# Pairing a group's quadrants by row instead of by token half, with a sixth seven-product group in the last pair

## The chip, the core and the metric

The kernel runs on one core of one Trainium2 chip. The metric is the device time of one execution in microseconds; the time before is the median of 3 runs.

## What is computed

A channel attention over 6016 tokens of 256 channels (its 256x256 probabilities are folded into the first weight), then two feed-forward layers with 2048 hidden columns, all in float32:

```python
s = (kn.T @ qn) / tau              # kn, qn: k and q normalized over the tokens
x = v @ softmax(s)                 # 6016 x 256
x = relu(x @ w_in1) ** 2 @ w_out1
out = leaky_relu(x @ w_in2, 0.01) @ w_out2
```

## The kernel before

**Products.** TensorE multiplies in fp32r. A float32 operand is split into a high part, cast by ScalarE, and a low part, which is the difference of operand and high part and is formed by VectorE (`low`, L109). One product is three matmuls (high by low, high by high, low by high; `mm3`, L541), all for one PSUM bank.

**Pairs and units.** The tokens are cut into six pairs of two halves, of 512 tokens each (448 in the fifth pair). In each layer and pair, eight units of 256 hidden columns follow: `(L, p, g)` is layer, pair, unit, and `n` numbers all 96 units. A unit's first multiplication (F1 to F7 in the banks ha and hb, L954) takes seven products instead of eight, as in Winograd's form of Strassen's algorithm. Its results lie in two tiles c, one for each token half, each with two rows of quadrants (fb 0 and 1: the two halves of the hidden columns).

**The second multiplication** has two forms. A plain unit casts each token half, forms its low part, and takes eight products, one for each half, fb and d (the two halves of the output channels). A unit of a seven-product group (`GROUPS`, L52; "S" in the code) takes seven, P1 to P7, and needs differences of quadrants (T1 to T4). P2, P3, P4 and P7 go into the four output banks y, P5 into a bank F (yF in the profile) and P1 and P6 into a bank A (yA). P6 (`yA<-b`) comes only when the P1 of its batch have been taken out of bank A; the batches are three or four units long (L963). Before the change the last pair has five seven-product units, 0 to 4; pairs 4 and 5 of layer 1 have six, and pairs 0 to 4 of layer 2 seven.

**VectorE and ScalarE in a unit of such a group** (`unit`, from L1585): casts and lows of G0 (1024 columns), B22 (512), G1 (1024), T3 (512) and T2 (512), and four differences of 512 columns (L1612): nine operations of VectorE.

**The order of the work** comes from a plan that the kernel makes when it is built (`build`, L987, and `simulate`, L814): every step is a task with an engine, a cost in units of one 512-column matmul, its dependencies and its buffers, and each engine takes the ready task that is due first. A transfer counts in the plan as its size over a rate (40 for the sums and the output) plus 14 units. TensorE (`class PE`, L889) takes the next first product when it is ready, and between two of them a given number of second products, the first ready ones of a list (L913). The list is filled by `mixed_items` (L1706): for unit g first what is late of unit g - 1 (P5, P4, P7), then the unit's own products; at the end of a batch its P6. The plan is written out as one fixed instruction order for each engine; SP's transfers are one queue in this order.

**The end.** In the last pair, the units that are at least two behind the last seven-product unit multiply their second half with the tokens on the output partitions (`second_by_tokens`, L577): 24 matmuls of 256 columns instead of 12 of 512. Before, these are units 6 and 7; unit 5 is plain. The shared sums of the second half must then be turned. `combine_last` (L1802) is issued with unit `BY_TOKENS - 1` (5 before): when the last P6 is done it adds bank A to the sums U, copies y(1,0) out as V, adds P5's bank, and adds the remaining banks; it transposes both results, stores them in DRAM (`ys`, L1834) and loads them back by token (`sums`, L1841). The first two plain products of that unit stand ahead of the late ones, but the one for y(1,0) has to wait for V. `finish_last` (L598) is the last work: four adds of the by-token banks and these sums (L552 in the profile), and three stores of the output. The other half's output is transposed and stored by four transfers (`put`, L621 and L627). The list's last part is sorted so that the by-token matmuls come last (L1872).

Of the kernel before, what the change touches and what calls it, by code (L numbers as in the profile page):

```python
# [19 lines left out]
P = 128  # L20
# [8 lines left out]
def attn_moe_moe2(  # L29
# [22 lines left out]
    GROUPS = {(1, 4): tuple(range(6)), (1, 5): tuple(range(6)), **{(2, p): tuple(range(7)) for p in range(5)}, (2, 5): tuple(range(5))}  # L52
# [43 lines left out]
    wi_d = {(L, g): dram.tile([P, 2, 8, P], F32, name=f"wi{L}_{g}") for L in (1, 2) for g in range(NG)}  # L96
# [27 lines left out]
    class Unit:  # L124
# [6 lines left out]
        def load(self):  # L131
            w, g = WS[self.kind, self.L], self.g
            t = cpool.tile([P, 2, 2 * P, 2], U32, tag="wst", name="wst", bufs=3)
            if self.kind == "i":
                src = w[:, g * 2 * P : (g + 1) * 2 * P].bitcast(U32).rearrange("(k p) f -> p k f", p=P)
            else:
                src = w[g * 2 * P : (g + 1) * 2 * P, :].bitcast(U32).rearrange("(b p) c -> p b c", p=P)
            nc.sync.dma_start(t.rearrange("p a b w -> p a (b w)"), src)
            self.w0, self.w1 = t[:, :, :, 0], t[:, :, :, 1]
# [28 lines left out]
        def into(self):  # L168

            if self.kind == "i" or self.blocks:  # L170
# [5 lines left out]
                return self.x, self.to[:, 0], self.to[:, 1]  # L176
# [21 lines left out]
        def store(self):  # L198
            if self.kind == "o":
                nc.sync.dma_start(wo_d[self.L, self.g], raw(self.to))  # L200
            elif self.L == 2:
                nc.sync.dma_start(wi_d[2, self.g][:, :, 1:], raw(self.to[:, :, 1:]))

    def sums(x, A11=1, A22=2, S1=4, S2=5, S3=6, S4=7):
# [8 lines left out]
    def out_sums(x):  # L213
        return sums(x, A11=2, A22=1, S1=5, S2=6, S3=7, S4=4)
# [355 lines left out]
    def second(n, half, fb, d):  # L570
# [3 lines left out]
        wo = both(wo_t[L, p, g], d, fb)  # L574
        mm3(y, wo, both(g_t[n, half], fb, slice(0, w)), begins((L, p, half, d)))

    def second_by_tokens(n, fb):  # L577
# [5 lines left out]
        for t in range(WIDTH[p] // P):  # L583
            if first:
                by_token.append(y_bank(L, p, 1, t) if t < KC else bank("ce"[t - KC], "y"))
            for m, (a, b) in enumerate(((0, 1), (0, 0), (1, 0))):
# [3 lines left out]
                    wo[:, b, :, fb],  # L590
# [44 lines left out]
    def shared(n, product, bank_key, first):  # L635
# [8 lines left out]
        else:  # L644
            a = both(late_w[n, "S2" if product == "P6" else "S3"], 0)
        x = {"P1": lambda: both(g_t[n, "G0"], 0, sl), "P2": lambda: both(g_t[n, "G0"], 1, sl),
             "P3": lambda: both(b_t[n, "B22"], sl), "P4": lambda: both(g_t[n, "G1"], 1, sl),
             "P5": lambda: both(g_t[n, "G1"], 0, sl), "P6": lambda: both(b_t[n, "T2"], sl),
             "P7": lambda: both(b_t[n, "T3"], sl)}[product]()
# [8 lines left out]

    def result(n, half, w, fb=None):
        c = c_t[n, half]  # L660
        return c[:, :, :w] if fb is None else c[:, fb, :w]
# [208 lines left out]
    KEEP = 8  # L870
    LATE_FIRST = True
# [9 lines left out]
    CONV_BEGIN, CONV_END = 1.4, 4  # L881
    N0 = 4
    FOLD_AFTER = "F1"
# [52 lines left out]
    A = {"A11": 1, "A22": 2, "A12": 3, "S1": 4, "S2": 5, "S3": 6, "S4": 7}  # L936
# [23 lines left out]
    FROM = {"P1": "G0", "P2": "G0", "P3": "B22", "P4": "G1", "P5": "G1", "P6": "T2", "P7": "T3"}  # L960
# [26 lines left out]
    def build(base):  # L987
# [33 lines left out]
        def convert(u, due, loaded=None, first=None, pace=4, begin=0):  # L1021
# [14 lines left out]
            if blocks:  # L1036
                raw_ = Buf("whl", 2, d(4))
                t = T("DVE", 3, d(4), u.high, deps=[t], alloc=raw_, uses=[w, cm])
                for i in range(4):
                    t = T("DVE", 1.1, d(4.2 + i / 10), lambda i=i: (sums if u.kind == "i" else out_sums)(u.x)[i](),  # L1040
                          deps=[t], uses=[raw_])
                to = Buf("wis", 1, d(5))
                t = T("ACT", 4.6, d(5), u.round, deps=[t], alloc=to, uses=[raw_])
                t = T("DVE", 5.2, d(6), u.low, deps=[t], uses=[raw_, to])
# [30 lines left out]
        def fold_sums(n, at_):  # L1075
# [19 lines left out]
            for i in range(4):  # L1095
                a = T("DVE", 1.1, at_ + 11 + i, lambda i=i: r["s"][i](), deps=[a], uses=[xb])
            h_ = T("ACT", 4.6, at_ + 16, lambda: nc.scalar.copy(wi_t[1, 0, g][:, 0], r["x"]), deps=[a], uses=[xb, b])
            lo = T("DVE", 5.2, at_ + 22, lambda: low(wi_t[1, 0, g][:, 1], r["x"], wi_t[1, 0, g][:, 0]), deps=[h_], uses=[xb, b])
            wi_ready[1, 0, g] = wi_ready[n + 1] = lo
            stores["i", 1, g, "s"] = T(  # L1100
                "SP", "wi", at_ + 30, lambda: nc.sync.dma_start(wi_d[1, g][:, :, 1:], raw(wi_t[1, 0, g][:, :, 1:])),
# [247 lines left out]
        def load_wi(n):  # L1349
            L, p, g = units[n]  # L1350
            b = wi_b[n] = Buf("wi", 3, base[n - 2] + 0.5)
            if n < 2 * NG and g < N0:
# [11 lines left out]
                def high():  # L1364
                    nc.scalar.copy(r["w"][:, 0, 4:], r["x"][:, 4:])

                def lows():
                    low(r["w"][:, 1, 4:], r["x"][:, 4:], r["w"][:, 0, 4:])

                def store():  # L1370
                    nc.sync.dma_start(wi_d[L, g][:, :, 4:], raw(r["w"][:, :, 4:]))
# [5 lines left out]
                for i in range(4):  # L1377
                    t = T("DVE", 1.1, e - 20 + i, lambda i=i: r["s"][i](), deps=[t], uses=[xb])
                t = T("ACT", 2.7, e - 10, high, deps=[t], uses=[xb, b])
                wi_ready[n] = T("DVE", 3, e - 5, lows, deps=[t], uses=[xb, b])  # L1380
                stores["i", 1, g, "s"] = T("SP", "fold", e, store, deps=[wi_ready[n]], uses=[b], lat=LOAD)
                return

            def load():
                nc.sync.dma_start(raw(wi_tile(L, p, g)[:, :, 1:]), wi_d[L, g][:, :, 1:])
# [4 lines left out]
        def wo_sums(n, ready, b):  # L1390
# [22 lines left out]
            for i in range(4):  # L1413
                t = T("DVE", 1.1, e + 1, lambda i=i: r["s"][i](), deps=[t], uses=[xb])
# [7 lines left out]
        def load_wo(n):  # L1422
# [24 lines left out]
            def load_s3():  # L1447
                t = late_w[n, "S3"] = wpool.tile([P, 2, 1, P], F32R, tag="ws", name="ws", bufs=3)
                nc.sync.dma_start(raw(t), sums_d[:, :, 7:])
# [3 lines left out]
            def load_s2():  # L1453
# [6 lines left out]
                nc.sync.dma_start(raw(late_w[n, "S2"]), sums_d[:, :, 6:7])  # L1460
# [18 lines left out]
        def unit(n):  # L1479
# [6 lines left out]
            h = lambda i: h_t[n, tags[i]][:, :w]  # L1486
            cb = [Buf("any" if is_mixed(L, p) else "c", 3, t0 + (5, 26)[half]) for half in range(2)]
            for half in range(2):
                cb[half].held = (90, 75)[half] if form == "S" else (55, 45)[half]
                c_tag[n, half] = cb[half]  # L1490
# [3 lines left out]
            def copy(where):  # L1494
# [3 lines left out]
                elif where == "C11":  # L1498
                    new_result(n, 0)
# [9 lines left out]
            def c22():  # L1509
                new_result(n, 1)  # L1510
# [12 lines left out]
            def c11_seeded():  # L1523
                new_result(n, 0)
# [6 lines left out]
            f = {}  # L1531

# [49 lines left out]
            c = lambda half, fb: result(n, half, w, fb)  # L1582
            _, turn_, _ = batch_of(n)

            def cast(name, half):  # L1585
                g_t[n, name] = gpool.tile([P, 2, 2, 512], F32R, tag="g", name="g")
                nc.scalar.copy(g_t[n, name][:, 0, :, :w], result(n, half, w))  # L1587

            def lows(name, half):
                gt = g_t[n, name]  # L1590
                low(gt[:, 1, :, :w], result(n, half, w), gt[:, 0, :, :w])

            def cast1(name, half, fb):
                if name == "B22":
                    b_t[n] = gpool.tile([P, 2, 2, 512], F32R, tag="g", name="b")
                    b_t[n, name] = b_t[n][:, 0]
                elif name == "T3":
                    b_t[n, name] = b_t[n][:, 1]
                elif turn_ > 1:
                    b_t[n, name] = cpool.tile([P, 2, 512], F32R, tag="whl", name="b")  # L1600
                else:
                    if turn_ == 0:
                        b_t[n, "pair"] = cpool.tile([P, 2, 2, 512], F32R, tag="wis", name="b", bufs=1)
                    b_t[n, name] = b_t[n - turn_, "pair"][:, turn_]
                nc.scalar.copy(b_t[n, name][:, 0, :w], c(half, fb))  # L1605

            def low1(name, half, fb):
                b = b_t[n, name]
                low(b[:, 1, :w], c(half, fb), b[:, 0, :w])

            def sub(to, a, b):
                tt(c(*to), c(*a), c(*b), op=ALU.subtract)  # L1612

            b = g_b[n, "G0"] = Buf("g", 4, t0 + 45)
            t = T("ACT", A2, t0 + 45, cast, "G0", 0, deps=[n11, n21], alloc=b, uses=[cb[0]])
            low_of[n, "G0"] = g0 = T("DVE", D2, t0 + 52, lows, "G0", 0, deps=[t], uses=[b, cb[0]])
            b = g_b[n, "B22"] = Buf("g", 4, t0 + 50)
            t = T("ACT", A1, t0 + 50, cast1, "B22", 1, 1, deps=[n12], alloc=b, uses=[cb[1]])
            low_of[n, "B22"] = b22 = T("DVE", D1, t0 + 57, low1, "B22", 1, 1, deps=[t], uses=[b, cb[1]])
            t1 = T("DVE", 3 * s, t0 + 59, sub, (0, 0), (1, 0), (0, 0), deps=[n22, g0], uses=cb)  # L1620
            t3 = T("DVE", 3 * s, t0 + 61, sub, (1, 0), (1, 1), (1, 0), deps=[n12, t1], uses=cb[1:])
            t2 = T("DVE", 3 * s, t0 + 65, sub, (1, 1), (1, 1), (0, 0), deps=[t3, b22], uses=cb)
            t4 = T("DVE", 3 * s, t0 + 67, sub, (0, 1), (0, 1), (1, 1), deps=[t2], uses=cb)
            b = g_b[n, "G1"] = Buf("g", 4, t0 + 74)
            t = T("ACT", A2, t0 + 74, cast, "G1", 0, deps=[t1, t4], alloc=b, uses=[cb[0]])
            low_of[n, "G1"] = T("DVE", D2, t0 + 84, lows, "G1", 0, deps=[t], uses=[b, cb[0]])
            b = g_b[n, "T3"] = g_b[n, "B22"]
# [316 lines left out]
```

## Time and profile before

| | |
|---|---|
| median of 3 runs | 1001.35 us (1000.79 to 1002.28) |
| the profiled execution | 1002.93 us |
| its span, first to last instruction | 1001.1 us |
| busy: TensorE, weight loads, VectorE, ScalarE | 994.6, 837.3, 901.4, 804.4 us |
| matmuls | 4528 |
| bytes moved | 234.97 MB, 235 GB/s over the span |

How to read it: times are microseconds from the span's start. PE is TensorE, PEld its weight loads, DVE VectorE, ACT ScalarE, SPq the queue of transfers that SyncE issues. A busy time is the union of an engine's instructions; matmuls overlap in the pipeline, so their pitch is read from start times. Tiles have the program's names: `y<-g,wo` is a second product, `ha<-x,wi` a first one.

### The profile page before, as it was taken

Reading aid. Unit: us, or ns where it says so; the run is one execution under the profiler, and the core shown is the slowest. Engines: PE = TensorE matmul, PEld = TensorE weight load, DVE = VectorE, ACT = ScalarE, POOL = GpSimd, SP = SyncE. Lnnn points to the kernel's source line nnn. Section 1 sums busy time; section 2 is a strip of 40 time slices with the busy share of each in tenths; the row PEclk is TensorE's granted clock in tenths of the full one; section 3 lists DMA queues with packets and bytes.
Section 4 is the critical chain, followed back from the end, with each engine's and each line's share of the span. In section 5 each row is a group of like instructions: output and inputs, shape, how many; then the busy total and the mean of one; then the engine's idle time right before and its main releaser. Section 6 shows DMA issues by size and latency. Waiting matters only on the chain.

```text
span 1001.1 us, 13148 instructions
## 1 busy us (share of the span) xinstructions
PE 994.6 (99%) x4528; PEld 837.3 (84%) x4528; DVE 901.4 (90%) x1314; ACT 804.4 (80%) x1184; POOL 0.7 (0%) x6
## 2 busy tenths in 40 slices
PE   9999999999999999999999999999999999999998
PEld 7888888887888888998888888888888888998887
DVE  4899999988988977999999999999999999998985
ACT  6799978877878777888898888779788788887773
POOL 0000000000000000000000000000000000000000
PEclk9999999999999999999999999999999999999999
DMA  9786559788978967965665665666577586676553
GB/s 339 281 253 205 200 193 287 266 308 296 332 284 294 318 249 265 316 219 206 223 209 200 229 215 202 201 217 226 172 219 233 182 239 227 210 233 220 195 143 84
DMA packets 160946, 234.97 MB, mean 235 GB/s; under 512 B 53232, under 2 KB 97264, under 8 KB 158576
## 3 DMA queue, kind: packets, MB, share of 16 engines
q1 hardware_dynamic: 160160, 233.48, 69.0%
q8 instruction: 36, 0.59, 0.2%
q10 hardware_dynamic: 720, 0.66, 0.2%
q14 instruction: 30, 0.25, 0.1%
HBM read 187.70 MB, written 46.40 MB: 234 GB/s over the span
## 4 chain that ended last, share of the span: by engine, by line
PE 97%; DMA 2%; DVE 0%; ACT 0%; ACTq 0%; issue 0%; SPq 0%
PE y L543 37%; PE ha L543 21%; PE hb L543 16%; PE yA L543 7%; PE yF L543 3%; PE hc L543 3%; PE sT L386 3%; PE he L543 2%; PE h L704 2%; PE pw L252 1%; DMA qk<-in_k_dram 1%; DMA qk<-in_q_dram 1%; PE y L587 0%; DVE o L552 0%; ACT e L472 0%; ACTq L338 0%
## 5 line engine op out<-in xcount | busy, mean ns | idle before, releaser
L543 PE MATMUL y<-g,wo 128*128 128x512 f32 (+1 forms) x1344 | 350.5, 387 | 0.0
L543 PEld LDWEIGHTS y<-g,wo 128*128 128x128 f32 x1344 | 252.1, 188 | 49.5 <-DVE wo L110 0.4
L543 PE MATMUL ha<-x,wi 128*128 128x512 f32 (+1 forms) x960 | 265.6, 385 | 0.0
L110 DVE TENSOR_TENSOR g<-c,g 128x1024 fp32r<-128x1024 f32 (+1 forms) x192 | 228.0, 1197 | 18.7 <-ACT g L674 13.9
L543 PEld LDWEIGHTS ha<-x,wi 128*128 128x128 f32 x960 | 180.0, 188 | 33.8 <-ACT c L1504 0.7
L543 PE MATMUL hb<-x,wi 128*128 128x512 f32 (+1 forms) x720 | 199.6, 386 | 0.1
L543 PEld LDWEIGHTS hb<-x,wi 128*128 128x128 f32 x720 | 134.3, 188 | 26.2 <-DVE c L550 1.7
L1612 DVE TENSOR_TENSOR c<-c 128x512 f32<-128x512 f32 (+1 forms) x208 | 139.9, 672 | 7.1 <-ACT c L691 1.2
L1587 ACT CAST g<-c 128x1024 fp32r<-128x1024 f32 (+1 forms) x104 | 105.2, 1023 | 5.1 <-PE y L543 2.4
L110 DVE TENSOR_TENSOR b<-c,b 128x512 fp32r<-128x512 f32 (+1 forms) x156 | 102.5, 668 | 2.0 <-ACT b L1605 1.7
L1605 ACT CAST b<-c 128x512 fp32r<-128x512 f32 (+1 forms) x156 | 93.1, 608 | 10.5 <-DVE c L1612 4.7
L681 ACT ACTIVATE c<-c 128x1024 f32<-128x1024 f32 (+1 forms) x96 | 100.0, 1043 | 1.5
L674 ACT CAST g<-c 128x1024 fp32r<-128x1024 f32 (+1 forms) x88 | 91.7, 1044 | 1.6
L1504 ACT COPY w<-ha 128x512 f32<-128x512 f32 (+1 forms) x80 | 46.2, 577 | 49.9 <-PE ha L543 49.6
L691 ACT ACTIVATE c<-c 128x512 f32<-128x512 f32 (+1 forms) x98 | 60.7, 621 | 8.8 <-DVE c L552 8.5
L1504 ACT COPY u<-ha 128x512 f32<-128x512 f32 (+1 forms) x80 | 46.0, 575 | 9.8 <-PE ha L543 6.9
L110 DVE TENSOR_TENSOR x<-xr,x 128x1024 fp32r<-128x1024 f32 (+3 forms) x47 | 49.1, 1051 | 0.6 <-ACT x L1261 0.6
L386 PE MATMUL sT<-qk 128*128 128x256 f32 x188 | 42.1, 382 | 1.4 <-DMA qk<-in_k_dram 1.3
L543 PE MATMUL yA<-g,wo 128*128 128x512 f32 (+1 forms) x156 | 42.9, 383 | 0.0
L543 PE MATMUL yF<-g,ws 128*128 128x512 f32 (+1 forms) x156 | 42.9, 383 | 0.0
L543 PE MATMUL y<-b,ws 128*128 128x512 f32 (+1 forms) x156 | 42.9, 383 | 0.0
L543 PE MATMUL y<-b,wo 128*128 128x512 f32 (+1 forms) x156 | 42.8, 383 | 0.0
(137 smaller groups left out, 1202.4 us busy)
## 6 DMA issues: line engine op xcount, KB each, us to landing
wi<-wi SPq DMA_DIRECT2D x88, 896.0 KB, 5.6
wo<-wo SPq DMA_DIRECT2D x84, 512.0 KB, 4.5
ws<-wo SPq DMA_DIRECT2D x120, 128.0 KB, 4.0
wst<-in_moe_w_in_dram SPq DMA_DIRECT2D x16, 512.0 KB, 6.0
wst<-in_moe_w_out_dram SPq DMA_DIRECT2D x16, 512.0 KB, 6.8
wi<-wis SPq DMA_DIRECT2D x8, 896.0 KB, 6.1
wo<-wis SPq DMA_DIRECT2D x7, 1024.0 KB, 7.6
wo<-wos SPq DMA_DIRECT2D x13, 512.0 KB, 5.8
```

What stands on the lines that cost most here:

```text
L110: tt(lo, x, raw(hi), op=ALU.subtract)
L252: nc.tensor.matmul(pw[:, i * 2 * P : (i + 1) * 2 * P], eT[:, a, j, i * P : (i + 1) * P], whl[g][:, b, j], start=t == 0 and (i == 0 or g == 0),
L386: nc.tensor.matmul(sT[j][:, :C], t[:, 0, i, j * P : (j + 1) * P], t[:, 1, i], start=n == 0 and i == 0, stop=last_tile and i == g - 1,)
L543: nc.tensor.matmul(ps, a[m], b[n], start=first and i == 0, stop=i == 2, skip_group_check=True)
L674: nc.scalar.copy(g_t[n, half][:, 0, :, :w], c)
L681: nc.scalar.activation(c, c, AF.Square)
L691: nc.scalar.activation(c, c, AF.Prelu, alpha=0.01)
L704: nc.tensor.matmul(h_t[n, half, fb][:, :w], a[i], b[j], start=start, stop=stop, skip_group_check=True)
L1504: nc.scalar.copy(to, h(0))
L1587: nc.scalar.copy(g_t[n, name][:, 0, :, :w], result(n, half, w))
L1605: nc.scalar.copy(b_t[n, name][:, 0, :w], c(half, fb))
L1612: tt(c(*to), c(*a), c(*b), op=ALU.subtract)
```

## The change

Quadrants are kept in tiles by row (fb) instead of by token half in units of seven-product groups. Then the three operands GA, GB and GC are whole tiles: GA serves P2 and P3, GB (after one difference, T3) P1 and P7, GC (after one difference of both quadrants with a broadcast T2) P4 and P5. T2 gets a temporary tile of its own, one buffer. VectorE has seven operations instead of nine, ScalarE four casts instead of five. To make this possible, output weights of such units are loaded with their two row blocks exchanged (two transfers instead of one). The weight sums S1 to S4 are formed by three operations instead of four, in other slots, and the input weights have seven blocks instead of eight, stored whole. The last pair gets a sixth such unit, by which unit 6 becomes the plain one and unit 7 alone is multiplied by tokens. The plan's begin and end of the weight conversion, the place of the fold and the order of P1 behind P2 and P3 change too.

```diff
-    GROUPS = {(1, 4): tuple(range(6)), (1, 5): tuple(range(6)), **{(2, p): tuple(range(7)) for p in range(5)}, (2, 5): tuple(range(5))}
+    GROUPS = {(1, 4): tuple(range(6)), (1, 5): tuple(range(6)), **{(2, p): tuple(range(7)) for p in range(5)}, (2, 5): tuple(range(6))}
...
-        wi_t[key] = wpool.tile([P, 2, 8, P], F32R, tag="wi", name="wi", bufs=3)
+        wi_t[key] = wpool.tile([P, 2, 7, P], F32R, tag="wi", name="wi", bufs=3)
...
+            to = t.rearrange("p a b w -> p a (b w)")
+            if turned(self.kind, self.L, g):
+                for b in range(2):
+                    nc.sync.dma_start(to[:, 1 - b], src[:, b])
+            else:
+                nc.sync.dma_start(to, src)
...
+        S2 = S3 + 1
         return [
             lambda: tt(x[:, S1], x[:, 0], x[:, A22], op=ALU.add),
-            lambda: tt(x[:, S3], x[:, A11], x[:, 0], op=ALU.subtract),
-            lambda: tt(x[:, S2], x[:, S1], x[:, A11], op=ALU.subtract),
+            lambda: tt(two(S3, S2), two(A11, S1), two(0, A11), op=ALU.subtract),
             lambda: tt(x[:, S4], x[:, 3], x[:, S2], op=ALU.subtract),
         ]
...
+    T2_BUFS = 1
...
-    CONV_BEGIN, CONV_END = 1.4, 4
+    CONV_BEGIN, CONV_END = 1.2, 4.3
     N0 = 4
-    FOLD_AFTER = "F1"
+    FOLD_AFTER = "F2"
...
-    FROM = {"P1": "G0", "P2": "G0", "P3": "B22", "P4": "G1", "P5": "G1", "P6": "T2", "P7": "T3"}
+    FROM = {"P1": "GB", "P2": "GA", "P3": "GA", "P4": "GC", "P5": "GC", "P6": "T2", "P7": "GB"}
+    PART = {"P1": 0, "P2": 0, "P3": 1, "P4": 0, "P5": 1, "P7": 1}
...
+            def t3():
+                c = result(n, 1, w)
+                tt(c[:, 1], result(n, 0, w)[:, 1], c[:, 1], op=ALU.subtract)
+
+            def t2():
+                c = result(n, 1, w)
+                s_t[n, "t2"] = tpool.tile([P, 1, 512], F32, tag="t2", name="t2", bufs=T2_BUFS)
+                tt(s_t[n, "t2"][:, 0, :w], c[:, 0], c[:, 1], op=ALU.add)
+
+            def t4_t1():
+                c = result(n, 0, w)
+                tt(c, c, s_t[n, "t2"][:, :, :w].to_broadcast([P, 2, w]), op=ALU.subtract)
...
+            b = g_b[n, "GA"] = Buf("g", 4, t0 + 45)
+            t = T("ACT", A2, t0 + 45, pair_cast, "GA", 0, deps=[n22, n21], alloc=b, uses=[ca])
+            low_of[n, "GA"] = ga = T("DVE", D2, t0 + 52, pair_low, "GA", 0, deps=[t], uses=[b, ca])
+            d3 = T("DVE", 3 * s, t0 + 50, t3, deps=[n22, n12, n11], uses=cb)
+            b = g_b[n, "GB"] = Buf("g", 4, t0 + 52)
+            t = T("ACT", A2, t0 + 52, pair_cast, "GB", 1, deps=[d3], alloc=b, uses=[cbb])
+            low_of[n, "GB"] = gb = T("DVE", D2, t0 + 58, pair_low, "GB", 1, deps=[t], uses=[b, cbb])
+            t2b = Buf("t2", T2_BUFS, t0 + 53)
+            d2 = T("DVE", 3 * s, t0 + 53, t2, deps=[d3], alloc=t2b, uses=[cbb])
+            d41 = T("DVE", D2, t0 + 54, t4_t1, deps=[ga, d2], uses=[ca, t2b])
+            b = g_b[n, "GC"] = Buf("g", 4, t0 + 74)
+            t = T("ACT", A2, t0 + 74, pair_cast, "GC", 0, deps=[d41], alloc=b, uses=[ca])
+            low_of[n, "GC"] = T("DVE", D2, t0 + 84, pair_low, "GC", 0, deps=[t], uses=[b, ca])
...
-                own = own if ends else [p1, *own]
+                own = own if ends else [*own, p1]
```

## Rows read from the trace of the kernel before

**Rows 1.** The page: busy time and share by engine, and granted clock by slice.

```profile
PE 994.6 (99%) x4528; PEld 837.3 (84%) x4528; DVE 901.4 (90%) x1314; ACT 804.4 (80%) x1184; POOL 0.7 (0%) x6
...
PEclk9999999999999999999999999999999999999999
```

**Rows 2.** Windows: busy us of PE, PEld, DVE, ACT, POOL; clock; DMA share, GB/s.

```profile
475.00:850.00 375.00, 375.00 (x1656) 310.36 (x1655) 354.85 (x480) 310.85 (x479) 0.00 (x0) 1.00 0.65 213
```

**Rows 3.** Groups of VectorE, shapes apart: busy us, mean ns, idle before.

```profile
L110 DVE TENSOR_TENSOR g<-c,g 128x1024 fp32r<-128x1024 f32 x160 | 193.7, 1219 | 18.3 <-ACT g L674 13.9 <-ACT g L1587 3.0
L1612 DVE TENSOR_TENSOR c<-c 128x512 f32<-128x512 f32 x156 | 107.6, 690 | 5.9 <-ACT c L691 1.2
L110 DVE TENSOR_TENSOR b<-c,b 128x512 fp32r<-128x512 f32 x117 | 78.8, 685 | 2.0 <-ACT b L1605 1.7
...
L207 DVE TENSOR_TENSOR wr<-wr 128x128 f32<-128x128 f32 x29 | 8.3, 286 | 0.2
...
L153 DVE SCALAR_TENSOR_TENSOR wr<-wst,cm 128x256 uint32<-128x256 uint32 x14 | 5.3, 420 | 0.2
```

**Rows 4.** Groups of ScalarE, shapes apart: the casts of a seven-product unit.

```profile
L1587 ACT CAST g<-c 128x1024 fp32r<-128x1024 f32 x78 | 81.0, 1050 | 4.8 <-PE y L543 2.3 <-DVE c L1612 1.5
L1605 ACT CAST b<-c 128x512 fp32r<-128x512 f32 x117 | 71.2, 621 | 6.9 <-DVE c L1612 2.2 <-PE y L543 1.1 <-PE yA L543 1.1
```

**Rows 5.** Timeline of TensorE, end of layer 1's last pair: start, us, instructions.

```profile
527.82 0.84 PE L543 MATMUL hb<-x,wi 128*128 128x512 f32 x3
528.50 0.84 PE L543 MATMUL yF<-g,ws 128*128 128x512 f32 x3
529.18 0.84 PE L543 MATMUL y<-g,wo 128*128 128x512 f32 x3
529.86 0.84 PE L543 MATMUL y<-b,ws 128*128 128x512 f32 x3
530.54 0.84 PE L543 MATMUL yA<-b,ws 128*128 128x512 f32 x3
531.22 0.84 PE L543 MATMUL ha<-x,wi 128*128 128x512 f32 x3
531.90 1.52 PE L543 MATMUL yA<-b,ws 128*128 128x512 f32 x6
```

**Rows 6.** Timeline of the end, all engines.

```profile
976.76 0.84 PE L543 MATMUL yA<-b,ws 128*128 128x512 f32 x3
...
984.24 7.64 PE L543 MATMUL y<-g,wo 128*128 128x512 f32 x33
...
985.72 2.00 SPq L1834 DMA_DIRECT2D ys<-o  x4
...
989.58 0.38 SPq L1841 DMA_DIRECT2D sums<-ys  x1
991.72 5.91 PE L587 MATMUL y<-wo,g 128*128 128x256 f32 x48
991.92 1.31 DVE L617 STREAM_TRANSPOSE o<-y 128x512 f32<-128x512 f32 x2 [2.65 <-PE y L543]
993.26 3.26 SPq L627 DMA_DIRECT2D out_dram<-o  x4
996.60 1.50 DVE L552 TENSOR_TENSOR o<-y,sums 128x256 f32<-128x256 f32 x4 [3.36 <-PE y L587]
```

**Rows 7.** Instructions on the tile sums: its transfer.

```profile
DMA to landing us min/median/max: 3.8/3.8/3.8
```

**Rows 8.** Chain of waits, end of the span: start, us, what.

```profile
991.88 4.69 PE y L587 x39
```

**Rows 9.** Timeline of TensorE while weights are converted.

```profile
240.91 0.84 PE L543 MATMUL y<-g,wo 128*128 128x512 f32 x3
241.69 0.96 PE L543 MATMUL ha<-x,wi 128*128 128x512 f32 x3
242.49 0.85 PE L543 MATMUL y<-g,wo 128*128 128x512 f32 x3
243.41 0.96 PE L543 MATMUL hb<-x,wi 128*128 128x512 f32 x3
```

**Rows 10.** Waits of SP's queue near the end: who, total us, times, longest.

```profile
SPq L1841 <- DMA ys<-o: 1.7, 1, 1.7
```

More of the change, by code (lines that the diff above doesn't have):

```diff
@@ L93, in attn_moe_moe2 @@
     eT = cpool.tile([P, 2, 8, P], F32R, tag="wis", name="eT", bufs=1).rearrange("p m (j a) c -> p m j (a c)", j=2 * KC)
-    wi_d = {(L, g): dram.tile([P, 2, 8, P], F32, name=f"wi{L}_{g}") for L in (1, 2) for g in range(NG)}
+    wi_d = {(L, g): dram.tile([P, 2, 7, P], F32, name=f"wi{L}_{g}") for L in (1, 2) for g in range(NG)}
     wo_d = {
@@ L175, in into @@
                     self.to = cpool.tile([P, 2, 8, P], F32R, tag="wis", name="wis", bufs=1)
-                return self.x, self.to[:, 0], self.to[:, 1]
+                k = 7 if self.L == 2 and self.kind == "i" else None
+                return self.x[:, :k], self.to[:, 0, :k], self.to[:, 1, :k]
             if self.L == 1:
@@ L213, in out_sums, with turned @@
     def out_sums(x):
-        return sums(x, A11=2, A22=1, S1=5, S2=6, S3=7, S4=4)
+        return sums(x, A11=2, A22=1, S1=5, S3=6, S4=4)
+    SUM_TIMES = 1.1, 1.8, 1.1
+    def turned(kind, L, g):
+        return kind == "o" and g in SG[L]
     v_t = {}
@@ L573, in second @@
         y = y_bank(L, p, half, d)[:, :w]
-        wo = both(wo_t[L, p, g], d, fb)
+        wo = both(wo_t[L, p, g], d, 1 - fb if turned("o", L, g) else fb)
         mm3(y, wo, both(g_t[n, half], fb, slice(0, w)), begins((L, p, half, d)))
@@ L645, in shared @@
             a = both(late_w[n, "S2" if product == "P6" else "S3"], 0)
[L646 to L649, printed above, removed]
+        x = both(b_t[n], sl) if product == "P6" else both(g_t[n, FROM[product]], PART[product], sl)
         if bank_key[0] == "y":
@@ L657, in shared, with by_fb @@
         mm3(y[:, :w], a, x, first)
+    def by_fb(n):
+        return is_mixed(*units[n][:2]) and form_of(n) == "S"
     def result(n, half, w, fb=None):
-        c = c_t[n, half]
-        return c[:, :, :w] if fb is None else c[:, fb, :w]
+        if fb is None:
+            return c_t[n, half][:, :, :w]
+        if by_fb(n):
+            half, fb = fb, half
+        return c_t[n, half][:, fb, :w]
     def new_result(n, half):
@@ L1038, in convert @@
                 t = T("DVE", 3, d(4), u.high, deps=[t], alloc=raw_, uses=[w, cm])
-                for i in range(4):
-                    t = T("DVE", 1.1, d(4.2 + i / 10), lambda i=i: (sums if u.kind == "i" else out_sums)(u.x)[i](),
+                for i in range(3):
+                    t = T("DVE", SUM_TIMES[i], d(4.2 + i / 10), lambda i=i: (sums if u.kind == "i" else out_sums)(u.x)[i](),
                           deps=[t], uses=[raw_])
                 to = Buf("wis", 1, d(5))
-                t = T("ACT", 4.6, d(5), u.round, deps=[t], alloc=to, uses=[raw_])
-                t = T("DVE", 5.2, d(6), u.low, deps=[t], uses=[raw_, to])
+                t = T("ACT", 4.1 if u.kind == "i" else 4.6, d(5), u.round, deps=[t], alloc=to, uses=[raw_])
+                t = T("DVE", 4.7 if u.kind == "i" else 5.2, d(6), u.low, deps=[t], uses=[raw_, to])
             else:
@@ L1376, in load_wi @@
                 t = T("DVE", 3, e - 25, join, deps=[t], alloc=xb, uses=[b])
[L1377 to L1381, printed above, removed]
+                for i in range(3):
+                    t = T("DVE", SUM_TIMES[i], e - 20 + i, lambda i=i: r["s"][i](), deps=[t], uses=[xb])
+                t = T("ACT", 3.2, e - 10, high, deps=[t], uses=[xb, b])
+                wi_ready[n] = T("DVE", 3.6, e - 5, lows, deps=[t], uses=[xb, b])
+                stores["i", 1, g, "s"] = T("SP", "wi", e, store, deps=[wi_ready[n]], uses=[b], lat=LOAD)
                 return
             def load():
-                nc.sync.dma_start(raw(wi_tile(L, p, g)[:, :, 1:]), wi_d[L, g][:, :, 1:])
+                nc.sync.dma_start(raw(wi_tile(L, p, g)), wi_d[L, g])
             dep = stores["i", 1, g, "s"] if L == 1 else stores["i", 2, g]
@@ L1412, in wo_sums @@
             t = T("DVE", 3, e, join, deps=[ready], alloc=xb, uses=[b])
-            for i in range(4):
-                t = T("DVE", 1.1, e + 1, lambda i=i: r["s"][i](), deps=[t], uses=[xb])
+            for i in range(3):
+                t = T("DVE", SUM_TIMES[i], e + 1, lambda i=i: r["s"][i](), deps=[t], uses=[xb])
             wb = Buf("wis", 1, e + 6)
@@ L1531, in unit @@
             f = {}
+            cq = (lambda half, fb: cb[1 - fb]) if by else (lambda half, fb: cb[half])
             def F_(name, deps):
@@ L1627, in unit, with low2 @@
-            b = g_b[n, "T3"] = g_b[n, "B22"]
-            t = T("ACT", A1, t0 + 80, cast1, "T3", 1, 0, deps=[t3, b22], uses=[b, cb[1]])
-            low_of[n, "T3"] = T("DVE", D1, t0 + 90, low1, "T3", 1, 0, deps=[t], uses=[b, cb[1]])
+                    b_t[n] = b_t[n - turn_, "pair"][:, turn_]
+                nc.scalar.copy(b_t[n][:, 0, :w], s_t[n, "t2"][:, 0, :w])
+            def low2():
+                low(b_t[n][:, 1, :w], s_t[n, "t2"][:, 0, :w], b_t[n][:, 0, :w])
+            ca, cbb = cb[1], cb[0]
```

105 lines of the change are left out of this document (43 added, 62 removed).

## The prediction

> **What bounds the kernel now.** I read the page's busy times first. TensorE is busy for 99% of the span at the full granted clock, VectorE for 90% [rows 1]. A busy share can flatter pipelined matmuls, so I then read starts. In a steady stage three matmuls of 512 columns start every 0.68 us and the next product follows at once, from whichever bank (529.86, 530.54, 531.22, 531.90 in [rows 5]): 0.227 us a matmul. From 475 to 850 us the stage is full in that sense, with VectorE at 354.85 of 375 us [rows 2]. So TensorE's instruction count sets the time, and work on VectorE and ScalarE is covered as long as no product waits for it. The few places where it does wait are in the first half, where weights are converted: around 241 us products start 0.78, 0.80 and 0.92 us apart [rows 9]. Counted over the timeline behind 62 us, such excess comes to some 2.3 us, 0.7 of it here.
>
> The end must be read by itself. The last matmuls, by tokens, end near 997.5; four adds from 996.60 put the sums read back from DRAM onto them and the output leaves [rows 6]. These adds wait for TensorE: the sums were asked for at 989.58 and took 3.8 us [rows 6, 7], so they were there at 993.4, 3.2 us before use. That slack is what a sixth group spends.
>
> **The arithmetic moved off VectorE.** A seven-product group now has, per unit of 512 tokens, two lows of 1.219 us, three lows of 0.685 and four differences of 0.690 [rows 3]: 2.44 + 2.06 + 2.76 = 7.26 us. After: three lows of 1024, one broadcast difference of 1024 (not in the trace; nearest row 1.219, ends 0.69 and 1.4 us; I take 1.22), two differences of 512, one low of 512: 3.66 + 1.22 + 1.38 + 0.69 = 6.95 us. ScalarE: two casts of 1.050 and three of 0.621 become three and one [rows 4], 3.96 to 3.77 us. The weight sums go from four operations of 0.286 to two of 0.286 and one of 256 columns at about 0.42 [rows 3], 1.14 to 0.99 us. Over some 52 units VectorE loses about 15 us of work. All of it lies beside TensorE [rows 2], so I cost it at **nothing**; if the cover is gone, a product waits, as in [rows 9]. It could take away those 2.3 us, and reordering could as well add as much: ends -2.3 and +2.3, taken 0. The conversion that starts earlier and ends later, the fold set one product later, the 13 output-weight loads split in two DMAs, the folded weights stored with seven blocks and the single temporary for T2 go with it; every such wait would show in TensorE's pitch.
>
> **The sixth group on TensorE.** In the last pair unit 5 needs 21 matmuls in the second multiplication, not 24: -3 x 0.227 = -0.68 us. Unit 6 no longer multiplies its second half by tokens: 24 matmuls of 256 columns at 4.69/39 = 0.120 us [rows 8] become 12 of 512: 2.72 - 2.89 = -0.17. Together **-0.85 us** on TensorE. The by-token matmuls are halved: they begin at 991.72 - 0.85 + 2.89 = 993.75, and the first tile of the last ones is complete at 996.60 - 0.85 = **995.75**.
>
> **The sums of the last pair.** Before the by-token banks can be taken, all shared sums must have been formed, transposed, stored and loaded back. The chain starts at the last P6. Before, that was unit 4's, at 976.76 (`yA<-b`), two units ahead of the end; the store is issued at 985.72 (8.96 us), the load at 989.58 (3.86 us), and it lands after 3.8: **16.6 us** [rows 6, 7]. Now the last P6 is unit 5's, and only one unit is left behind it. Where does it run? In both earlier pairs with six groups the list is the same: in the second of them the last unit's F6 starts at 527.82 and the three P6 run at 530.54, 531.90 and 532.58 [rows 5], so behind all first products of the pair. In the last pair there remain behind the last P6 the plain products of units 6 and 7, 8 + 4, less those that ran ahead of it; I take one ahead, since only one stands ahead of the P6 in the list and needs no sum. So the P6 starts (1 + 11) x 0.68 us before 993.75: **985.59**, by 0.68 either way per product.
>
> From there I work forward. At the least the store needs the product's 0.84, two products that wait for the copy of a bank (1.36), six operations of about 0.69 in a row (add, copy, add, transpose, add, transpose; [rows 3, 6]) and some eight handovers of 0.12: 7.3 us. At the most, as before, 8.96. So the store is issued between 992.9 and 994.55. If the load follows as before (3.86 + 3.8), the sums land at 1000.55 to 1002.2. SP waits in place: the load sat there until the store had landed [rows 10]. The four stores of the other half's output, issued behind the load now (993.26, for 3.26 us, right behind two transposes at 991.92; [rows 6]), become ready at 993.95 + 1.31 = 995.26, while the plan in the kernel reckons with 12.8 + 14 of its units of 0.227 us, 6.1 us, from store to load. So they may come ahead of it: then the load goes at 998.55 and lands at 1002.35. Between 1000.55 and 1002.35 I take the middle, **1001.45**. Nothing else on TensorE is held up: the banks are free 0.7 us and more before the store, near 993.
>
> The Trainium skill, DMA: Bandwidth & Descriptors, section Anatomy of one DMA, gives a transfer about 2.0 us fixed and bytes over 436 GB/s, and says that a semaphore wait is the issuing sequencer's. By its figures the load of 512 KB would take an estimated 3.2 us and the total come out 0.6 us lower; the row has 3.8, and goes into the sum. For the wait in SP's place the trace agrees [rows 10].
>
> **Sum.** The adds start at 1001.45 instead of 996.60: +4.85 us, which holds TensorE's -0.85 already. Rest of the end unchanged, body 0. The profiled execution (1002.93 us, span 1001.1) becomes 1007.8; it stood 1.58 us above the median 1001.35. Median: **1006.2 us**.
>
> **Rivals.**
> *The last P6 runs early (0.20).* If P5, P4 and P7 of unit 5 are not ready in time, the list lets the P6 pass; they need only unit 5's P1 and one add. It decides at 995.75 - 15.0 = 980.7 for the start of the last P6 (15.0 being 7.3 + 3.86 + 3.8): then the sums are in time, TensorE sets the end, and the time is 1001.35 - 0.85 = 1000.5, no change. Every us later costs one. Against it: in [rows 5] P7 went ahead of the P6, and VectorE now finishes those operands sooner.
> *The body gets denser (0.14).* P6 early as above and the waits of [rows 9] gone: 1000.5 less 1.2 to 2.3, so 998.2 to 999.3; faster. For it: fewer operations where VectorE is fullest. Against: it needs both.
> *VectorE is the bound (0.02 of the chance above).* Then 52 x 0.31 = 16 us would come off: 985. The unbroken pitch [rows 5] speaks against. The Trainium skill, Perfetto Trace Analysis, section Identifying the Most-Contended Engine, calls matmul busy time no good measure and asks for weight-load time; here that is 84% [rows 1] against VectorE's 90%, and by that reading this rival would win. The pitch decides.
> *A new wait in each unit (0.05).* GB now waits for a difference of two rows, and one T2 temporary serves all. One product's slot, 0.23 us a matmul, in each of 52 units: +12 us, 1013.
> *The sums late, as forecast (0.61).*
>
> **How the numbers follow.** A measurement of this kernel tells about 0.2%, 2.0 us, from no change: 999.35 to 1003.35. Slower: the forecast, of which I give 0.01 to its lower end inside that band, and the new wait: 0.65. Same: 0.21 with the early P6. Faster: 0.14. The forecast's own range is P6 at 984.9 with the short chain (sums at 999.9, +3.3: 1004.6) to 986.3 with output ahead and the full chain (about 1003, +6.4: 1007.7), give or take part of the body's 2.3. The range that holds 8 in 10 reaches down to the early P6 and the first of the denser body, and leaves out the new wait and the rest: 999.0 to 1008.4.
>
> **What would show it.** Right: the last `yA<-b` within a us of 985.6; the store of the sums at 993 to 994.5; VectorE's last adds released by a DMA and not by TensorE, with TensorE idle over 4 us before the end; TensorE's last matmul near 996.6; VectorE's busy time down by some 10 us with the pitch unchanged. Wrong: the adds still released by TensorE, or gaps in TensorE's pitch in the units of layer 2.

## The result, and the profile after

The changed kernel takes 1006.67 us (1006.41 to 1009.94), the kernel before 1001.75 us over six runs: a ratio of 1.0055, with a 95% interval of 1.0042 to 1.0069. It is **slower by 4.9 us**, where 1006.2 was forecast (+4.85). The profiled execution took 1006.68 us, with a span of 1004.9.

The page's first part, busy us by engine, and how often:

```profile
PE 992.3 (99%) x4513; PEld 836.4 (83%) x4513; DVE 893.7 (89%) x1190; ACT 795.8 (79%) x1138; POOL 0.7 (0%) x6
```

Against [rows 1]: 15 matmuls fewer, as counted (three of the second multiplication in unit 5, and 24 that became 12 in unit 6), VectorE down by 7.7 us, ScalarE by 8.6. All of it is shorter, and the kernel is longer. So I go to the end, with the timeline of all engines:

```profile
982.56 0.84 PE L557 MATMUL yA<-b,ws 128*128 128x512 f32 x3
983.24 0.84 PE L557 MATMUL y<-g,wo 128*128 128x512 f32 x3
983.92 1.52 PE L557 MATMUL yA<-b,ws 128*128 128x512 f32 x6
...
985.28 7.72 PE L557 MATMUL y<-g,wo 128*128 128x512 f32 x33
...
992.12 2.00 SPq L1861 DMA_DIRECT2D ys<-o  x4
992.84 3.03 PE L601 MATMUL y<-wo,g 128*128 128x256 f32 x24
...
995.99 0.38 SPq L1868 DMA_DIRECT2D sums<-ys  x1
996.48 2.58 SPq L641 DMA_DIRECT2D out_dram<-o  x4
1000.44 1.42 DVE L566 TENSOR_TENSOR o<-y,sums 128x256 f32<-128x256 f32 x4 [6.09 <-DMA sums<-ys]
```

Read it against [rows 6] from below. The four last adds were released by TensorE at 996.60; now a DMA releases them, at 1000.44, after 6.09 us in which VectorE had nothing else. TensorE's last matmul had ended near 995.9 and the first tile was complete before 995: what stands in between is the way of the sums. Upward from there: the load is issued at 995.99, the store at 992.12, and the last P6 starts at 983.92 + 0.68 = **984.60** instead of 976.76. Behind it come exactly the 11 plain products of the forecast (x33) before the by-token matmuls. Behind the adds nothing changed: 4.48 us to the end of the span before, 4.46 now.

The tile of the sums: its load's time from issue to landing, before 3.8 us [rows 7]:

```profile
DMA to landing us min/median/max: 4.3/4.3/4.3
```

The operations of VectorE that replaced the rest of [rows 3], groups with shapes apart (L1629 is the broadcast difference, L1625 T2, L1620 T3, L218 the paired weight sums):

```profile
L1629 DVE TENSOR_TENSOR c<-c,t 128x1024 f32<-128x1024 f32 x40 | 48.9, 1223 | 1.1
...
L1625 DVE TENSOR_TENSOR t<-c 128x512 f32<-128x512 f32 x40 | 27.6, 691 | 1.1
L1620 DVE TENSOR_TENSOR c<-c 128x512 f32<-128x512 f32 x40 | 27.4, 685 | 2.9 <-ACT c L708 2.4
...
L218 DVE TENSOR_TENSOR wr<-wr 128x256 f32<-128x256 f32 x29 | 12.3, 425 | 0.9
```

They cost what the rows of before said: 1.223 us for the broadcast (1.22 taken), 0.425 for 256 columns (0.42). So the longer time does not come from the price of an operation.

### The profile page after: what moved, and what is told of

Its sections match the earlier page's. It is cut to its first block, busy times and chain, and to the rows that moved or that the text cites. A ratio compares the mean times of both kernels' runs of the same rounds, so it can differ in the third digit from the quotient of the medians.

```text
span 1004.9 us, 12973 instructions
## 1 busy us (share of the span) xinstructions
PE 992.3 (99%) x4513; PEld 836.4 (83%) x4513; DVE 893.7 (89%) x1190; ACT 795.8 (79%) x1138; POOL 0.7 (0%) x6
## 4 chain that ended last, share of the span: by engine, by line
PE 93%; DMA 4%; DVE 1%; ACT 1%; issue 1%; SPq 0%; ACTq 0%; DVEq 0%
PE y L557 35%; PE ha L557 21%; PE hb L557 16%; PE yA L557 7%; PE yF L557 3%; PE hc L557 3%; PE sT L400 3%; PE h L721 2%; PE he L557 2%; PE pw L266 1%; DMA qk<-in_k_dram 1%; DMA wos<-wis 1%; DMA wst<-in_moe_w_out_dram 1%; DMA qk<-in_q_dram 1%; DMA sums<-ys 0%
## 5 line engine op out<-in xcount | busy, mean ns | idle before, releaser
L557 PE MATMUL y<-g,wo 128*128 128x512 f32 (+1 forms) x1497 | 391.9, 386 | 0.0
L557 PEld LDWEIGHTS y<-g,wo 128*128 128x128 f32 x1497 | 280.8, 188 | 54.1 <-DVE y L566 0.2
L110 DVE TENSOR_TENSOR g<-c,g 128x1024 fp32r<-128x1024 f32 (+1 forms) x245 | 290.7, 1195 | 24.0 <-ACT g L691 11.1
L1612 ACT CAST g<-c 128x1024 fp32r<-128x1024 f32 (+1 forms) x159 | 161.7, 1025 | 13.7 <-PE y L557 7.4
L691 ACT CAST g<-c 128x1024 fp32r<-128x1024 f32 (+1 forms) x86 | 89.7, 1044 | 3.1 <-PE y L557 1.2
L1629 DVE TENSOR_TENSOR c<-c,t 128x1024 f32<-128x1024 f32 (+1 forms) x53 | 63.1, 1190 | 1.2
L557 PE MATMUL y<-g,ws 128*128 128x512 f32 (+1 forms) x159 | 43.7, 383 | 0.0
L1280 ACT CAST x<-xr 128x1024 fp32r<-128x1024 f32 (+3 forms) x44 | 40.3, 929 | 1.3 <-PE ha L557 0.9
L400 PEld LDWEIGHTS sT<-qk 128*128 128x128 f32 x188 | 35.5, 191 | 6.8 <-issue 2.0
L557 PE MATMUL yA<-b,ws 128*128 128x512 f32 (+1 forms) x159 | 41.1, 383 | 0.0
```

The lines of the kernel that those rows point to most:

```text
L110: tt(lo, x, raw(hi), op=ALU.subtract)
L400: nc.tensor.matmul(sT[j][:, :C], t[:, 0, i, j * P : (j + 1) * P], t[:, 1, i], start=n == 0 and i == 0, stop=last_tile and i == g - 1,)
L557: nc.tensor.matmul(ps, a[m], b[n], start=first and i == 0, stop=i == 2, skip_group_check=True)
L691: nc.scalar.copy(g_t[n, half][:, 0, :, :w], c)
L1280: nc.scalar.copy(part(0), src())
L1612: nc.scalar.copy(g_t[n, name][:, 0, :, :w], result(n, i, w))
```

## The experiments

Theory: the sixth group leaves too little work behind the last P6 to cover the sums' way through DRAM. Rivals: the pairing by row costs the time, or something else at the end does. Medians, and the ratio to the kernel before on the same chip. The runs lie on several chips, where the kernel before took 1001.05 to 1001.76 us, so a difference between two of these medians is good to some 0.7 us:

| kernel | us | ratio, 95% interval |
|---|---|---|
| changed kernel, five units in the last pair | 1002.34 | 1.0011 (1.0002 to 1.0020) |
| kernel before, six units | 1007.11 | 1.0058 (1.0044 to 1.0071) |
| changed, adds take other data | 1003.15 | 1.0019 (1.0009 to 1.0028) |
| changed, last P6 first | 1005.99 | 1.0047 (1.0033 to 1.0061) |
| changed, last P7 and P6 first | 1004.98 | 1.0038 (1.0024 to 1.0051) |
| changed, sums turned by TensorE | 1003.73 | 1.0023 (1.0014 to 1.0032) |
| five units, VectorE work added | 1004.88 | 1.0037 (1.0023 to 1.0050) |
| the same, in the plan too | 1004.62 | 1.0033 (1.0023 to 1.0044) |
| five units, conversion placed as before | 1004.47 | 1.0027 (1.0017 to 1.0036) |
| before, conversion placed as after | 1003.05 | 1.0018 (1.0009 to 1.0027) |

**The sixth group undone.**

```diff
-(2, 5): tuple(range(6))}
+(2, 5): tuple(range(5))}
```

> The changed kernel with five seven-product units in the last pair again, all else kept. Theory (the sums of the last pair come too late): one unit more stands behind the last P6, the four last adds are released by TensorE again, near 995.7 us, 4.7 us earlier than with six; 1001 to 1002.5 us. Rival (the pairing by row, with its new order of VectorE's work, costs the time): still 1005.5 to 1007 us.

1002.34 us. The timeline of its end:

```profile
974.99 0.84 PE L557 MATMUL yA<-b,ws 128*128 128x512 f32 x3
...
984.63 2.01 SPq L1861 DMA_DIRECT2D ys<-o  x4
988.54 0.38 SPq L1868 DMA_DIRECT2D sums<-ys  x1
989.95 5.91 PE L601 MATMUL y<-wo,g 128*128 128x256 f32 x48
...
994.83 1.50 DVE L566 TENSOR_TENSOR o<-y,sums 128x256 f32<-128x256 f32 x4 [3.36 <-PE y L601]
```

The last P6 is 9.6 us earlier than in the changed kernel, TensorE releases the adds again, and the time lies in the theory's range. The rival falls: of the 4.9 us, the sixth group makes 4.3.

**The sixth group alone**, in the kernel before.

```diff
-(2, 5): tuple(range(5))}
+(2, 5): tuple(range(6))}
```

> The kernel before with six seven-product units in the last pair, nothing else. Theory (late sums): the last adds wait for the sums' load, as in the changed kernel; 1005 to 1008 us. Rival (pairing by row costs the time): TensorE has 0.85 us less to do and sets the end; 1000.5 to 1001.2 us.

1007.11 us, with the same picture: the timeline of its end.

```profile
982.65 1.52 PE L543 MATMUL yA<-b,ws 128*128 128x512 f32 x6
...
991.67 2.02 SPq L1834 DMA_DIRECT2D ys<-o  x4
...
995.48 0.38 SPq L1841 DMA_DIRECT2D sums<-ys  x1
...
999.99 1.42 DVE L552 TENSOR_TENSOR o<-y,sums 128x256 f32<-128x256 f32 x4 [6.78 <-DMA sums<-ys]
```

From both sides, then: the sixth group costs 4.3 us with the pairing by row and 6.1 without it; the pairing by itself costs about one us with five units and nothing with six (1.0055 and 1.0058).

**Other data for the last adds.**

```diff
...
-                nc.sync.dma_start(last_sums["t"], ys_d.rearrange("(t p) c -> p t c", p=P))
+                nc.sync.dma_start(last_sums["t"], x2_d[0][:, :2].rearrange("p a (b c) -> p (a b) c", c=C))
...
-            done[L, p, 1, "all"] = [T("SP", "wo", t0 + 61, load, deps=[t], alloc=b)]
+            done[L, p, 1, "all"] = [T("SP", "wo", t0 + 30, load, deps=[got["P1"]], alloc=b)]
```

> The changed kernel, but the last adds take other data: the tile is loaded from layer 1's stored output, early, instead of from the stored sums, so the output's second half of the last pair is not the layer's. The sums are still formed, transposed and stored. Theory (only the way of the sums through DRAM sets the end): the adds start when the first by-token tile is complete, near 994.9 us, 5.5 us earlier; 1001 to 1002 us. Rival (something else at the end, such as the output stores behind them or VectorE's last work): 1005 us or more.

1003.15 us, above the theory's range and below the rival's: 3.5 us of the 5.5 came back. The timeline shows why not all:

```profile
976.15 0.59 SPq L1868 DMA_DIRECT2D sums<-x  x1
...
992.97 2.03 SPq L1861 DMA_DIRECT2D ys<-o  x4
993.90 3.03 PE L601 MATMUL y<-wo,g 128*128 128x256 f32 x24
...
996.87 1.42 DVE L566 TENSOR_TENSOR o<-y,sums 128x256 f32<-128x256 f32 x4 [1.45 <-DMA ys<-o]
```

The adds no longer wait for the load, but for the *store* of the sums to land: it reads a buffer that the adds' output takes over, a wait that stood hidden behind the load. It is worth about 1 us (the first tile is complete near 995.9). And TensorE arrived 1.06 us later (993.90, not 992.84): in the first half ScalarE had waited 3.4 us for a load of output weights, and TensorE 1.6 for ScalarE (2.1 and 0.6 in the profile of the changed kernel). Together these are the 2.0 us by which the adds of this execution came behind the expected 994.9.

**The last P6 first.** In the last pair P1 goes ahead of P2 and P3, and the three last P6 to the front of unit 6's list; then the last P7 as well.

```diff
-                own = own if ends else [*own, p1]
+                own = own if ends else [p1, *own] if (L, p) == (2, NP - 1) else [*own, p1]
...
+                front = p6 if ends_all else []
-                items.extend([*own[:2], *late, *([p7] if late else []), *p6, *own[2:]])
+                items.extend([*front, *own[:2], *late, *([p7] if late else []), *([] if front else p6), *own[2:]])
```

> The changed kernel with P1 ahead of P2 and P3 in the last pair and the last three P6 at the front of unit 6's list. Theory (the last P6's start sets the end): the last P6 starts at 981.9 to 983.5 us instead of 984.6, and every us of it comes off the time: 1004 to 1005.6 us, with the adds still waiting for the load. Rival (the end is set by SP's queue or by the load alone, whenever the P6 runs): 1006 to 1007 us.

1005.99 us, between the two ranges. The last P6 started at 981.95, 2.65 us earlier, as expected, but the store only 0.97 earlier. The timeline of its end, with ScalarE's copy of y(1,0):

```profile
981.27 1.52 PE L557 MATMUL yA<-b,ws 128*128 128x512 f32 x6
...
984.67 0.84 PE L557 MATMUL y<-g,ws 128*128 128x512 f32 x3
...
985.54 0.59 ACT L1712 COPY acc<-y 128x512 f32<-128x512 f32 x1 [2.49 <-PE y L557]
...
986.17 0.69 DVE L566 TENSOR_TENSOR acc<-acc 128x512 f32<-128x512 f32 x1 [2.65 <-ACT acc L1712]
...
991.15 2.01 SPq L1862 DMA_DIRECT2D ys<-o  x4
...
992.28 2.56 PE L557 MATMUL y<-g,wo 128*128 128x512 f32 x10 [1.56 <-DVE g L110]
...
994.68 3.03 PE L601 MATMUL y<-wo,g 128*128 128x256 f32 x24
...
999.30 1.42 DVE L566 TENSOR_TENSOR o<-y,sums 128x256 f32<-128x256 f32 x4 [3.11 <-DMA sums<-ys]
```

The copy needs the last P7 (`y<-g,ws`) too, and P7 now stood behind; VectorE's next add waited 2.7 us for the copy. So "the start of the last P6" was half of the condition. TensorE itself lost 1.6 us to a late low of VectorE, and its by-token matmuls began 1.84 us later than in the changed kernel; the adds still started 1.14 us earlier, since they waited for the load. With P7 ahead of the P6:

```diff
-                front = p6 if ends_all else []
-                items.extend([*front, *own[:2], *late, *([p7] if late else []), *([] if front else p6), *own[2:]])
+                front = [p7, *p6] if ends_all else []
+                items.extend([*front, *own[:2], *late, *([] if front or not late else [p7]), *([] if front else p6), *own[2:]])
```

> As e4_p6_first, where the sums' chain then waited for the copy of y(1,0), which stands behind the last P7; here the last P7 goes to the front too, ahead of the P6. Theory (the later of the last P6 and the last P7 starts the chain, then 7.5 us to the store): the last P6 at about 982.6 us, the store near 990.1 instead of 992.1: 1004.2 to 1005.3 us. Rival (the store cannot come earlier because the adds need unit 6's plain products, and their lows are late): 1005.8 us or more, as e4_p6_first.

1004.98 us, within the theory's range. Its end:

```profile
980.25 0.84 PE L557 MATMUL y<-g,ws 128*128 128x512 f32 x3
...
982.29 2.20 PE L557 MATMUL yA<-b,ws 128*128 128x512 f32 x9
...
984.45 0.56 ACT L1712 COPY acc<-y 128x512 f32<-128x512 f32 x1
...
990.72 2.01 SPq L1862 DMA_DIRECT2D ys<-o  x4
...
994.61 0.38 SPq L1869 DMA_DIRECT2D sums<-ys  x1
...
999.14 1.42 DVE L566 TENSOR_TENSOR o<-y,sums 128x256 f32<-128x256 f32 x4 [3.77 <-DMA sums<-ys]
```

The store is 1.4 us earlier than in the changed kernel, the adds 1.3, the time 1.7. The last of the three P6 started at 983.65 (1.36 us behind the first, at 982.29), a us later than the expected 982.6: in TensorE's fixed order two first products stand between it and P7. Bank A did not hold it: VectorE had taken the last P1 out by 977.07.

**No round trip.** Eight transposes on TensorE put the sums into two free banks, ScalarE copies them out; the store, the load and two transposes on VectorE go.

```diff
...
+            def turn():
+                for i in range(2):
+                    last_sums[i] = bank("ab"[i], "turn")
+                for t in range(4):
+                    for d, which in enumerate("VU"):
+                        at_ = t % 2 * C + d * P
+                        nc.tensor.transpose(last_sums[t // 2][:, at_ : at_ + P], S(which)[:, t * P : (t + 1) * P], ident)
...
```

> The changed kernel, but the sums of the last pair are turned by eight transposes on TensorE into two banks and copied by ScalarE, so the store, the load and VectorE's two transposes go. Theory (the round trip through DRAM makes the sums late): the adds are released by TensorE again. TensorE gets eight transposes of about 0.13 us, 1.0 us; the first tile is complete near 995.9 us instead of sums landing at 1000.4: 1001.5 to 1002.9 us, about level with five units. Rival (late P6 costs TensorE time too, since the by-token banks come free late): 1004 us or more.

1003.73 us: three of the five us are back with all six groups kept, though the median lies 0.8 us above the expected range (its profiled execution, 1002.62 us, lies in it). The timeline:

```profile
992.72 1.03 PE L1677 MATMUL turn<-ident,acc 128*128 128x128 f32 x8
...
993.36 1.08 ACT L1682 COPY sums<-turn 128x512 f32<-128x512 f32 x2 [7.58 <-PE turn L1677]
993.51 3.12 PE L601 MATMUL y<-wo,g 128*128 128x256 f32 x24
...
995.65 1.49 DVE L566 TENSOR_TENSOR o<-y,sums 128x256 f32<-128x256 f32 x4 [1.41 <-issue]
```

No transfer releases the adds, and they start 4.8 us earlier than in the changed kernel; from there to the end of the span it takes 5.2 us instead of 4.46. The turn took TensorE 0.79 us (992.72 to 993.51), about what the sixth group saved; so it is no gain over five groups.

**Is VectorE's work free?** One more operation of 128 columns in each seven-product unit, in the kernel with five units:

```diff
                 tt(s_t[n, "t2"][:, 0, :w], c[:, 0], c[:, 1], op=ALU.add)
+                tt(s_t[n, "t2"][:, 0, :P], c[:, 0, :P], c[:, 1, :P], op=ALU.add)
```

> The kernel with five units in the last pair (e1_five) with one more VectorE operation of 128 columns in each of the 52 seven-product units (it forms the first quarter of T2 again), some 15 us of work, as much as the pairing by row took away. Theory (VectorE's work is covered by TensorE): 1001.3 to 1003.5 us, as e1_five. Rival (VectorE is the bound, or next to it): all of it shows, 1010 us or more.

1004.88 us: 2.5 us for 12.1 us more of VectorE's busy time (889.7 to 901.8). Neither range. The windows of the stage from 475 to 850 us, first with five units alone, then with the added operation:

```profile
475.00:850.00 375.00, 375.00 (x1658) 310.81 (x1657) 349.23 (x415) 306.40 (x449) 0.00 (x0) 1.00 0.66 213
```

```profile
475.00:850.00 375.00, 374.89 (x1649) 308.34 (x1648) 355.55 (x446) 305.16 (x446) 0.00 (x0) 1.00 0.67 211
```

Busy time of TensorE hides it, the count tells it: nine matmuls fewer in the same stretch, 2.0 us. The plan did not know of that operation, so I let it know.

```diff
-            d2 = T("DVE", 3 * s, t0 + 53, t2, deps=[d3], alloc=t2b, uses=[cbb])
+            d2 = T("DVE", 4.3 * s, t0 + 53, t2, deps=[d3], alloc=t2b, uses=[cbb])
```

> As e6_more_vector, but the plan reckons with the added operation: T2's cost there is 4.3 units instead of 3. Theory (work that the plan knows is covered; e6 lost because its order didn't reckon with it): 1001.5 to 1003.3 us, as e1_five, with some 1657 matmuls between 475 and 850 us. Rival (VectorE's cover is simply used up at some 355 of 375 us): 1004.3 to 1006 us, with some 1650 matmuls.

1004.62 us, and 1646 matmuls in that stage, as the rival had it:

```profile
475.00:850.00 375.00, 373.78 (x1646) 308.10 (x1645) 355.43 (x447) 305.28 (x446) 0.00 (x0) 1.00 0.66 212
```

So letting the plan know brought nothing back. The two losses are not the same, though. About 1.2 us of this one, five of the twelve matmuls, fall at one place, where the new plan has put a load (`xr<-x`) later in SP's queue: VectorE waits for the load, ScalarE for VectorE, and TensorE for a copy of ScalarE. The timeline there:

```profile
541.27 1.23 DVE L1289 TENSOR_TENSOR xr<-xr 128x1024 f32<-128x1024 f32 x1 [2.04 <-DMA xr<-x]
...
544.29 0.97 PE L557 MATMUL hb<-x,wi 128*128 128x512 f32 x3 [1.01 <-ACT hb L1526]
```

And the rival does not hold as it stands: the kernel before keeps the full pitch with as much VectorE work there, 354.85 us and 1656 matmuls [rows 2]. With the pairing by row the pitch was full at 349 us of VectorE's work and no longer at 355, so its shorter VectorE time is no spare time. Why it needs it is not shown. Its operands depend on later results (a whole row instead of one quadrant), and the added operation not only fills VectorE but stands between T2 and GC in every unit, so that P4 and P5 get their operand later; no run separates these.

**Where the conversion stands.** The kernel with five units, with the old place of the conversion, and the kernel before with the new one:

```diff
-    CONV_BEGIN, CONV_END = 1.2, 4.3
+    CONV_BEGIN, CONV_END = 1.4, 4
```

> The kernel with five units in the last pair (e1_five), with the weight conversion planned between the same points as before the change (1.4 to 4 pairs instead of 1.2 to 4.3). Theory (what e1_five lost against before, some 1 us, comes from conversion loads that land late in the new place, near 237 us, and stop ScalarE and then TensorE): ScalarE's wait for the load of the output weights near 237 us is gone, 1000.5 to 1001.7 us. Rival (the loss lies elsewhere, as in the split loads or the reordered VectorE work): 1002 to 1003 us.

> The kernel before, with the conversion between the new points (1.2 to 4.3) and nothing else. Theory (the new place of the conversion costs): slower than before by 0.5 to 1.5 us. Rival (it costs nothing or helps by spreading the work): 1000.3 to 1001.5 us, level with before or below.

1004.47 and 1003.05 us. The first misses both ranges; the second is slower than before by 0.9 to 2.7 us, with a median 1.9 above, over the theory's 1.5. Each plan got worse by leaving the setting that it had (the first 1.0027 against 1.0011, with intervals that just overlap), so neither place is good in itself. ScalarE's wait near 237 us was indeed gone in the first (its waits for transfers between 100 and 420 us name other tiles, 1.4 us at most), and the time did not follow. Its profile shows where it lost instead. From 62 to 350 us both kernels with five units have 1304 matmuls; in the windows from 350 to 450 us, first with the new place of the conversion, then with the old one, ten are missing, about 2 us:

```profile
350.00:450.00 100.00, 100.00 (x472) 88.12 (x471) 87.14 (x122) 82.20 (x117) 0.00 (x0) 1.00 0.74 256
```

```profile
350.00:450.00 100.00, 99.54 (x462) 85.92 (x461) 84.37 (x115) 80.96 (x114) 0.00 (x0) 1.00 0.77 260
```

Why five units with the pairing by row take one us more than before stays **open**: profiles show one execution each, and such differences lie between executions. One part is the same in several of them: from the last adds to the end of the span, five units with the pairing by row take 4.9 to 5.05 us (four kernels), five with the old pairing 4.5 (two kernels), though the last store of the output lands 3.6 us behind the adds in all six.

## Why the prediction was right

*TensorE sets the end, before.* Right, and five units in the changed kernel show it again.

*TensorE's -0.85 us.* The count is exact. The by-token matmuls began at 992.84 instead of 993.75, since this execution began the feed-forward layers 0.53 us earlier (first `h<-x,wi` at 52.42, before at 52.95) and lost some 0.4 us less from there on.

*The last P6.* 985.59 was forecast, 984.60 measured; from it to the by-token matmuls 12 products, as counted.

*From P6 to store.* Between 7.3 and 8.96 us; measured 7.52, near the lower bound, but not by its terms. The eight handovers of 0.12 us stand in no row, and this path does not show them: the first add starts 0.04 us behind the P6's end, the store 0.03 behind the last transpose. Nor do two products that wait for the copy lie in this path. In their place VectorE does more than counted: from 985.48 to 992.09 it runs nine operations with no gap over 0.11 us, six adds, two transposes and a low that stands among them. That the sum came within 0.3 us is luck. VectorE's first, second and last operation there:

```profile
985.48 0.69 DVE L566 TENSOR_TENSOR acc<-acc,yA 128x512 f32<-128x512 f32 x1 [0.60 <-PE yA L557]
986.08 1.22 DVE L110 TENSOR_TENSOR g<-c,g 128x1024 fp32r<-128x1024 f32 x1
...
991.38 0.71 DVE L631 STREAM_TRANSPOSE o<-acc 128x512 f32<-128x512 f32 x1
```

*From store to load, and the load.* 3.87 us, as before. It landed after 4.3 instead of 3.8. The Trainium skill, DMA: Bandwidth & Descriptors, section Anatomy of one DMA, would have it an estimated 3.2, by a figure that it gives for transfers issued by GpSimd; this one is SP's, and no run here agrees: they show 3.8 to 4.4.

*The output's stores ahead of the load.* They did not come ahead. Their issue (996.48) stayed behind it (995.99). The sum took the middle between this case and the shortest chain, 0.9 us above the latter.

*Sum.* The adds started at 1000.44, 1.0 us ahead of the forecast: 0.99 from the earlier P6 and 0.90 from the middle that was taken, less 0.22 up to the store, 0.01 up to the load and 0.65 from the load's issue to the adds (4.45 us, not 3.8). So the store came at 992.12, ahead of the 993 to 994.5 that was named as a sign, and errors of both signs met. In the profiled executions the adds moved by 3.84 us (4.85 forecast) and the time by 3.75. That the median moved by 4.92 and the forecast came within 0.5 us is partly chance: the profiled execution of before stood 1.2 us above the median of its six other runs.

*VectorE at nothing.* Right for the sum, wrong as a rule: -7.7 us of its work gave no time, but +12 us cost 2.5. Some 10 us less were named; with five units it is 11.7 less, and the sixth group adds 4.0 again. The step "all of it lies beside TensorE" holds for the kernel before and needed a look at how little room was left.

*Rivals.* The P6 did not run early: 984.60 against the deciding 980.7. The denser body did not come: the 0.4 us above are far from 1.2 to 2.3, and from 62 to 475 us, where [rows 9] lie, there are 1884 matmuls, before 1883. Nor did the new wait per unit: from 475 to 850 us it is 1657, before 1656. The Trainium skill, Perfetto Trace Analysis, section Identifying the Most-Contended Engine, would have pointed to VectorE by the weight-load time (84% against 90%); taking 11.7 us off VectorE, with five units (901.4 to 889.7), brought nothing, so the pitch was the better witness here.

## What to carry to other kernels

Where a pipelined kernel ends in a chain that goes through DRAM, count the work that stands behind the chain's *first* link, and compare it with the chain's length: 16.6 us of chain had 3.2 us of slack, and starting it 9.6 us later cost more than the 0.85 us that this saved. Work behind that link moves the end of the bottleneck engine, not of the chain: with the last P6 first, TensorE's last matmuls came 1.84 us later and the adds 1.14 us earlier. When a wait is removed, name the one behind it first: here a store's buffer, then P7's copy.

## What was not expected

Sums that were loaded while four output stores were issued behind them within 1.2 us took 4.1 to 4.4 us to land (four kernels); where those stores came 2.9 us or more behind, 3.8 and 3.9 (six kernels). ScalarE waited for a load of output weights between 235 and 238 us in all nine kernels with the new place of the conversion, one of them with the old pairing, for 0.5 to 3.4 us, and in none of the three with the old place. Six of the nine differ in the last pair alone. The two longest waits, 3.4 and 3.1 us, were followed by ones of 1.6 and 1.3 on TensorE.
